# A fused attention and two-layer kernel: four output accumulators in step with the first product, transposes back on TensorE, batch 0 in quarters

## The chip, the cores and the metric

One core of a Trainium2 chip. The time is the device time of one execution in microseconds, as a median of several runs; beside it stands the span of a profiled execution, from the first to the last instruction.

## The reference, cut to what matters

```
B, H, S, Ns, D = 8, 8, 512, 32, 64          # x: B,H,S,D   state: B,H,Ns,D
scores  = x @ state^T / sqrt(D);  a  = softmax(scores)    # over the 32 states
xread   = a @ state
scores2 = state @ x^T / sqrt(D);  a2 = softmax(scores2)   # over the 512 rows
sread   = a2 @ x
rows    = concat(xread, sread) per batch -> (B*(S+Ns), H*D) = (4352, 512)
h = rows @ w_in                              # 512 -> 2048
g = 0.5*h*(1+erf(h/sqrt(2)))                 # exact gelu
out = g @ w_out                              # 2048 -> 512, float32
```

Inputs are float32, the kernel computes in bf16 with float32 accumulation. The kernel takes the softmax without subtracting the maximum.

## The kernel before, in words

Each batch has 512 x rows and 32 state rows. For the x rows the kernel never forms `xread`. It multiplies the state of a batch with `w_in` once (P, 256 x 2048, `pmat`, in four column blocks `f` of 512) and uses h = A P, where A is the softmax of the scores of all heads (512 x 256). `mm1(b, m)` makes 128 of the 2048 columns of h for all 512 rows (two matmuls of 512 columns) and ScalarE takes the gelu into `g`. The second product is cut into units of four matmuls: for one group j of 128 output rows and one quarter q of the 2048, so 16 units (`mm2`) a batch; after the quarter q = 3 DVE copies the bank out (`evac`) and SP stores 256 KB.

Attention of a batch: `rearr` puts x into `x4` (two heads side by side), x^T is made (`xT`), `scores` multiplies it with the block-diagonal state `sbd`, ScalarE takes exp into `e`, `norm` on DVE divides by the sum over states into `a`, and A^T (`AT`) is made. x^T and A^T come from TensorE transposes with a DVE copy (`xtr`, `atr`) for batches 0 and 1 and from transposing DMAs on SP (`xtr_dma`, `atr_dma`) for batches 2 to 7. `sread` multiplies e with x and with a column of ones, 64 matmuls of a 32x64 or 32x1 result; DVE divides; `srt` transposes the result into `XSR`. When all batches are through, `mm1_sr` and `mm2_sr` take the 256 state rows of all batches through the two products.

The order is written by hand. Batch 0 runs its attention in two halves with `keep_warm` matmuls in its gaps. Then a loop runs over 8 batches of 16 steps; step s runs what `extra` or `steady` list for it (the attention of the next batch and its P, two blocks at a time), then `mm1(b, s)`, then one `mm2` unit, 16 steps behind (`lag = 16`). So no unit runs during batch 0, and only two output banks are open at a time, one group j after another. The last eight units come after the state rows.

PSUM has eight banks. Pool `ps_f` has six of them, for everything but the output; `ps_o` has two, for the output and the warming matmuls. Each engine runs its own instructions in the order of the program. Weights, state and x of batches 1 to 7 come through POOL's software descriptors with a cast to bf16; x of batch 0 comes as float32 over SP and ACT in four pieces. Tiles `xb` have three buffers, so x of batch b + 3 is asked for when batch b has been rearranged.

Of the kernel before, what the change touches and what calls it, by code (L numbers as in the profile page):

```python
# [17 lines left out]
def kernel(  # L18
# [25 lines left out]
    ps_f = ctx.enter_context(tc.tile_pool(name="ps_f", bufs=6, space=bass.MemoryType.PSUM))  # L44
    ps_o = ctx.enter_context(tc.tile_pool(name="ps_o", bufs=2, space=bass.MemoryType.PSUM))
# [7 lines left out]
    ident = persist.tile([128, 128], BF16, name="ident")  # L53
    sbd = persist.tile([128, B, HC, 2 * NS], BF16, name="sbd")
# [4 lines left out]
    x0f = persist.tile([128, 2, HC, SJ * D], FP32, name="x0f")  # L59
    warm = persist.tile([128, 512], BF16, name="warm")  # L60
    ones = persist.tile([128, 1], BF16, name="ones")
    x4s = [persist.tile([128, SJ, HC, 128], BF16, name=f"x4_{i}") for i in range(2)]
# [5 lines left out]
    for c in range(HC):  # L68
        eng = nc.sync if c % 2 == 0 else nc.scalar
        eng.dma_start(out=x0f[:, :, c, :], in_=x0_rows[:, :, c, :])  # L70

    make_identity(nc, ident)
    nc.vector.memset(warm, 0.0)  # L73
    nc.gpsimd.memset(sbd, 0.0)
    nc.gpsimd.memset(ones, 1.0)
# [22 lines left out]
    load_w_in(0)  # L98
    load_w_in(1)
# [5 lines left out]
    load_w_in(2)  # L105
    load_w_in(3)
    load_w_out(0)
    load_w_out(1)
    load_x(2)
    load_w_out(2)  # L110
    load_w_out(3)
# [3 lines left out]
    def keep_warm(n):  # L115
        ps = ps_o.tile([128, 512], FP32, name="warm_ps", tag="op")
        for _ in range(n):
            nc.tensor.matmul(ps, lhsT=warm[:, 0:128], rhs=warm, start=True, stop=True)  # L118

# [25 lines left out]
    def begin(b):  # L145
        A = Att()
        atts[b] = A
        A.x4 = x4s[b % 2]
        A.xT = att.tile([128, SJ, HC, 128], BF16, name="xT", tag="xT")
        A.e = att.tile([128, SJ * 2, HC * NS], BF16, name="e", tag="e")  # L150
        A.a = att.tile([128, SJ * 2, HC * NS], BF16, name="a", tag="a")

    def rearr(b):
        A = atts[b]
        eng = nc.vector if b < 3 else nc.gpsimd
        for t in range(2):
            eng.tensor_copy(  # L157
                out=A.x4[:, :, :, 64 * t:64 + 64 * t].rearrange("p j c d -> p c j d"),
                in_=xbs[b][:, 4 * t:4 * t + 4, :].rearrange("p c (j d) -> p c j d", d=D),
            )  # L160

    def rearr0(c):
        A = atts[0]
        nc.vector.tensor_copy(
            out=A.x4[:, :, c, :].rearrange("p j (t d) -> p t j d", t=2),
            in_=x0f[:, :, c, :].rearrange("p t (j d) -> p t j d", d=D),
        )

    def xtr0(c):
        A = atts[0]  # L170
        ps = ps_f.tile([128, SJ, 128], BF16, name="xT_ps", tag="f")
        for j in range(SJ):
            nc.tensor.transpose(ps[:, j, :], A.x4[:, j, c, :], ident)
        nc.scalar.copy(out=A.xT[:, :, c, :], in_=ps)

    def xtr(b, half):
        A = atts[b]
        ps = ps_f.tile([128, 2, SJ, 128], BF16, name="xT_ps", tag="f")
        for ci in range(2):
            for j in range(SJ):  # L180
                nc.tensor.transpose(ps[:, ci, j, :], A.x4[:, j, 2 * half + ci, :], ident)
        nc.vector.tensor_copy(out=A.xT[:, :, 2 * half:2 * half + 2, :].rearrange("p j c n -> p c j n"), in_=ps)

    def score_mms(b, c):
        A = atts[b]
        if c % 2 == 0:
            A.pt = ps_f.tile([128, SJ, 2, 2, NS], FP32, name="pt", tag="f")
        for j in range(SJ):
            nc.tensor.matmul(  # L189
                A.pt[:, j, :, c % 2, :],  # L190
                lhsT=A.xT[:, j, c, :],
                rhs=sbd[:, b, c, :],
                start=True,
                stop=True,
            )

    def expo(b, half):
        A = atts[b]
        nc.scalar.activation(  # L199
            out=A.e[:, :, 64 * half:64 * half + 64],  # L200
            in_=A.pt.rearrange("p j t c n -> p (j t) (c n)"),
# [3 lines left out]

    def xtr_dma(b):
        A = atts[b]
        nc.sync.dma_start_transpose(
            out=A.xT.rearrange("p j c n -> p (j c) n"), in_=A.x4.rearrange("p j c n -> p (j c n)")
        )  # L210

    def scores(b, half):
        score_mms(b, 2 * half)
        score_mms(b, 2 * half + 1)
        expo(b, half)
# [17 lines left out]
    def atr(b):  # L233
        A = atts[b]
        A.AT = att.tile([128, SJ, 2, 128], BF16, name="AT", tag="AT")
        if b == 0:
            for t in range(2):
# [3 lines left out]
                o, i = A.AT[:, :, t, :], ps  # L241
# [9 lines left out]
        nc.vector.tensor_copy(out=A.AT.rearrange("p j t n -> p t j n"), in_=ps)  # L251

    def atr_dma(b):
        A = atts[b]
        A.AT = att.tile([128, SJ, 2, 128], BF16, name="AT", tag="AT")
        nc.sync.dma_start_transpose(
            out=A.AT.rearrange("p j t n -> p (j t) n"), in_=A.a
        )


    def sread(b):
        A = atts[b]
        sr = ps_f.tile([128, 130], FP32, name="sr", tag="f")
        for o, n in ((0, D), (128, 1)):
            for t in range(2):
                for j in range(SJ):
                    for c in range(HC):
                        q = slice(32 * c, 32 * c + 32)
                        nc.tensor.matmul(  # L269
                            sr[q, o + n * t:o + n * t + n],  # L270
                            lhsT=A.e[:, 2 * j + t, q],
                            rhs=A.x4[:, j, c, 64 * t:64 * t + 64] if n == D else ones,
                            start=(j == 0),
                            stop=(j == SJ - 1),
                        )
        A.srm = att.tile([128, 2, D], BF16, name="srm", tag="srm")
        inv = att.tile([128, 2], FP32, name="inv", tag="inv")
        nc.vector.reciprocal(out=inv, in_=sr[:, 128:130])
        nc.vector.tensor_tensor(
            out=A.srm,  # L280
            in0=sr[:, 0:128].rearrange("q (t d) -> q t d", t=2),
            in1=inv[:, :].to_broadcast((128, 2, D)),
            op=ALU.mult,
        )

    def srt(b):
        A = atts[b]
        ps = ps_f.tile([128, HC, NS], BF16, name="srT", tag="f")
        nc.tensor.transpose(
            ps.rearrange("p c n -> p (c n)"), A.srm.rearrange("q t d -> q (t d)"), ident  # L290
        )
# [4 lines left out]
    def pmat(b, fs, act=()):  # L296
        if b not in Ps:
            Ps[b] = att.tile([128, 2, d_ff], BF16, name="P", tag="P")
        pss = []
        for f in fs:  # L300
            ps = [ps_f.tile([128, 512], FP32, name="p_ps", tag="f") for t in range(2)]
            for c in range(HC):
                for t in range(2):
                    nc.tensor.matmul(  # L304
                        ps[t][32 * c:32 * c + 32, :],
                        lhsT=sbd[64 * t:64 * t + 64, b, c, 32 * t:32 * t + 32],
                        rhs=w_in_bf[64 * t:64 * t + 64, c, f * 512:(f + 1) * 512],
                        start=True,
                        stop=True,
                    )  # L310
            pss.append(ps)
        for f, ps in zip(fs, pss):
            for t in range(2):
                dst = Ps[b][:, t, f * 512:(f + 1) * 512]
                if (f, t) in act:
                    nc.scalar.copy(out=dst, in_=ps[t])  # L316
                else:
                    nc.vector.tensor_copy(out=dst, in_=ps[t])  # L318
# [4 lines left out]
    def mm1(b, m):  # L323
# [3 lines left out]
        for t in range(2):  # L327
# [3 lines left out]
                rhs=atts[b].AT[:, :, t, :],  # L331
# [20 lines left out]
    def mm2(u):  # L352
        b, r = u // 16, u % 16
        if b == 0:
            j, q = 2 * (r // 8) + r % 2, (r % 8) // 2
        else:
            j, q = r // 4, r % 4
        if q == 0:
            ops[j % 2] = ps_o.tile([128, d_model], FP32, name="op", tag="op")
        ps = ops[j % 2]  # L360
# [8 lines left out]
        if q == 3:  # L369
            rows = out[b * SB:b * SB + S, :].rearrange("(p j) n -> j p n", j=SJ)[j]  # L370
            evac(ps, [(rows, slice(0, 128))], last=(u == 16 * B - 1))
# [13 lines left out]
    def mm2_sr(s):  # L385
        ps = ps_o.tile([128, d_model], FP32, name="ops", tag="op")
# [18 lines left out]
    for c in range(HC):  # L405
        rearr0(c)
    xtr0(0)
    xtr0(1)
    score_mms(0, 0)
    xtr0(2)  # L410
    score_mms(0, 1)
    expo(0, 0)
    xtr0(3)
    score_mms(0, 2)
    keep_warm(2)
    score_mms(0, 3)
    expo(0, 1)
    norm(0, 0)
    norm(0, 1)
    keep_warm(6)  # L420
    pmat(0, (0,), act=((0, 0), (0, 1)))
    keep_warm(4)
    atr(0)
    keep_warm(2)

    extra = {
        0: {
            1: [lambda: pmat(0, (1,))],
            3: [lambda: state_prep(1, B)],
            5: [lambda: begin(1), lambda: rearr(1), lambda: xtr(1, 0)],  # L430
            6: [lambda: xtr(1, 1), lambda: scores(1, 0), lambda: scores(1, 1)],
            7: [lambda: pmat(0, (2,))],
            8: [lambda: norm(1, 0), lambda: norm(1, 1)],
            10: [lambda: pmat(0, (3,))],
            12: [lambda: pmat(1, (0,))],
            13: [lambda: atr(1)],
            14: [lambda: pmat(1, (1,))],
        },
        1: {
            1: [lambda: sread(0), lambda: pmat(1, (2,))],  # L440
            2: [lambda: srt(0)],
# [87 lines left out]
```

## Time and profile before

| | |
|---|---|
| median of 3 runs | 237.99 us (236.87 to 240.91) |
| profiled execution | 236.87 us |
| its span | 234.7 us |
| granted clock | 0.999 |
| first `mm1` starts | 14.59 us |
| first `mm2` unit starts | 31.45 us |
| last output copy starts | 230.70 us |

The page gives the busy time of each engine, the chain of work that ended last, the costliest groups of instructions, and the DMA issues. PE is TensorE's matmuls, PEld its weight loads, DVE VectorE, ACT ScalarE, POOL GpSimd, SP the queue of the sync engine. In a group, `out<-in` names the tiles; the number after `|` is busy time and mean of one; the last column is idle time ahead of it and what ended it. Three groups to know:

```profile
L335 ACT ACTIVATE g<-hp 128x512 bf16<-128x512 f32 x128 | 74.5, 602 | 61.9 <-PE hp L328 61.7
L318 DVE CAST P<-p_ps 128x512 bf16<-128x512 f32 x38 | 24.3, 684 | 11.1 <-PE p_ps L304 11.1
L376 PE MATMUL hps<-XSR,w_in_bf 128*128 128x256 bf16 x64 | 8.5, 273 | 0.0
```

The mean of a matmul is its length from first column to result; matmuls overlap, so what it costs in a dense row is the distance between starts.

### The profile page before, as it was taken

To read this page: it belongs to the slowest core of one execution; us is meant where nothing else is said; L and a number is where in the kernel's file an instruction comes from. 1 tells how busy PE (TensorE), PEld (TensorE's weight loads), DVE (VectorE), ACT (ScalarE), POOL (GpSimd) and SP (SyncE) were. 2 spreads that over 40 slices of the span, in tenths; PEclk is the share of its full clock that TensorE was granted. 3 is DMA by queue.
4 is the path that set the end of the run, shared out by engine and by line. 5 is a ranking of instruction groups with operands and counts; after the bars stand their busy time and mean duration, and the time that the engine had idled before them with its cause. 6 is when DMAs were issued, how large, how long until landed. Compare 5 with 4: busy or idle time off the path is not lost.

```text
span 234.7 us, 4315 instructions
## 1 busy us (share of the span) xinstructions
PE 217.1 (92%) x1844; PEld 100.7 (43%) x1844; DVE 85.3 (36%) x162; ACT 124.7 (53%) x208; POOL 28.1 (12%) x38
## 2 busy tenths in 40 slices
PE   5996799889979999999799999999999999999993
PEld 1543244434334444444344444444444444567441
DVE  2655974274135413631181317231623111111120
ACT  2577754485467446744494549454955454426000
POOL 8745001304000400030002000000000000000000
PEclk9999999999999999999999999999999999999999
DMA  7999999972923294252804061316131111211122
GB/s 205 149 178 206 202 205 185 126 161 26 226 76 86 56 165 98 62 75 53 128 0 106 31 143 38 89 47 134 46 92 45 47 45 55 80 46 47 27 65 87
DMA packets 38707, 23.12 MB, mean 98 GB/s; under 512 B 21920, under 2 KB 34464, under 8 KB 38688
## 3 DMA queue, kind: packets, MB, share of 16 engines
q0 software_dynamic: 13376, 8.09, 25.3%
q1 hardware_dynamic: 24352, 14.03, 24.8%
q10 hardware_dynamic: 960, 0.72, 1.0%
q8 instruction: 14, 0.23, 0.4%
q14 instruction: 5, 0.04, 0.1%
HBM read 17.30 MB, written 8.91 MB: 112 GB/s over the span
## 4 chain that ended last, share of the span: by engine, by line
PE 68%; DMA 18%; DVE 5%; ACT 3%; POOL 3%; issue 1%; SPq 1%; POOLq 0%; ACTq 0%
PE op L362 37%; PE hp L328 18%; DMA xT<-x 13%; DMA xb<-in_x_dram 5%; PE hps L376 3%; PE ops L388 3%; PE p_ps L304 3%; PE sr L269 2%; PE pt L189 2%; ACT g L335 2%; DVE osb L348 1%; POOL w_in_bf L79 1%; DVE P L318 1%; DVE a L226 1%; DVE cs L223 1%
## 5 line engine op out<-in xcount | busy, mean ns | idle before, releaser
L362 PE MATMUL op<-w_out_bf,g 128*128 128x512 bf16 x512 | 130.2, 379 | 0.0
L335 ACT ACTIVATE g<-hp 128x512 bf16<-128x512 f32 x128 | 74.5, 602 | 61.9 <-PE hp L328 61.7
L328 PE MATMUL hp<-AT,P 128*128 128x512 bf16 x256 | 75.9, 380 | 2.9 <-DVE P L318 1.5
L362 PEld LDWEIGHTS <-g 128*128 128x128 bf16 x512 | 50.1, 98 | 58.7
L348 DVE COPY osb<-op 128x512 f32<-128x512 f32 x31 | 21.4, 690 | 88.8 <-PE op L362 88.8
L328 PEld LDWEIGHTS <-P 128*128 128x128 bf16 x256 | 22.5, 98 | 30.2 <-issue 6.6
L318 DVE CAST P<-p_ps 128x512 bf16<-128x512 f32 x38 | 24.3, 684 | 11.1 <-PE p_ps L304 11.1
L157 POOL COPY x<-xb 128x1024 bf16<-128x1024 bf16 x10 | 10.1, 1044 | 93.3 <-PE sr L269 76.9
L316 ACT CAST P<-p_ps 128x512 bf16<-128x512 f32 x26 | 14.1, 601 | 6.1 <-PE p_ps L304 6.1
L223 DVE TENSOR_REDUCE cs<-e 128x16 f32<-128x512 bf16 x16 | 10.9, 682 | 17.2 <-ACT e L199 17.2
L199 ACT ACT_TABLE_LOAD x7 | 9.0, 1283 | 9.7 <-PE pt L189 9.7
L189 PE MATMUL pt<-sbd,xT 128*128 128x64 bf16 x128 | 6.3, 200 | 6.2 <-DMA xT<-x 5.4
L304 PE MATMUL p_ps<-w_in_bf,sbd 64*32 64x512 bf16 x256 | 11.9, 384 | 0.1
L226 DVE TENSOR_TENSOR a<-e,ics 128x512 bf16<-128x512 bf16 x16 | 11.1, 692 | 0.6
L383 ACT ACTIVATE g_sr<-hps 128x256 bf16<-128x256 f32 x16 | 6.1, 384 | 8.4 <-PE hps L376 8.0
L335 ACT ACT_TABLE_LOAD x8 | 10.3, 1283 | 0.1
L189 PEld LDWEIGHTS <-xT 128*128 128x128 bf16 x128 | 4.9, 102 | 10.5 <-DMA xT<-x 8.4
L199 ACT ACTIVATE e<-pt 128x512 bf16<-128x512 f32 x16 | 8.8, 595 | 0.7 <-PE pt L189 0.6
L118 PE MATMUL warm_ps<-warm 128*128 128x512 bf16 x20 | 7.9, 542 | 1.2 <-DVE warm L73 1.2
L376 PE MATMUL hps<-XSR,w_in_bf 128*128 128x256 bf16 x64 | 8.5, 273 | 0.0
L345 ACT COPY osb<-op 128x256 f32<-128x256 f32 x1 | 0.4, 372 | 13.9 <-DVE osb L343 13.9
L376 PEld LDWEIGHTS <-w_in_bf 128*128 128x128 bf16 x64 | 6.3, 98 | 2.7
(48 smaller groups left out, 81.8 us busy)
## 6 DMA issues: line engine op xcount, KB each, us to landing
out_dram<-osb SPq DMA_DIRECT2D x31, 256.0 KB, 2.3
xb<-in_x_dram POOLq DMA_DIRECT2D x7, 512.0 KB, 11.6
w_in_bf<-in_moe_w_in_dram POOLq DMA_DIRECT2D x8, 256.0 KB, 10.1
w_out_bf<-in_moe_w_out_dram POOLq DMA_DIRECT2D x4, 512.0 KB, 14.9
x0f<-in_x_dram SPq DMA_DIRECT2D x2, 256.0 KB, 3.4
x0f<-in_x_dram ACTq DMA_DIRECT2D x2, 256.0 KB, 4.3
out_dram<-osb SPq DMA_DIRECT2D x8, 64.0 KB, 1.7
st_bf<-in_state_dram POOLq DMA_DIRECT2D x1, 224.0 KB, 10.2
```

Of the source, the lines that this page charges most:

```text
L189: nc.tensor.matmul(A.pt[:, j, :, c % 2, :], lhsT=A.xT[:, j, c, :], rhs=sbd[:, b, c, :], start=True, stop=True,)
L199: nc.scalar.activation(out=A.e[:, :, 64 * half:64 * half + 64], in_=A.pt.rearrange("p j t c n -> p (j t) (c n)"), func=AF.Exp, scale=scale,)
L223: nc.vector.reduce_sum(out=cs, in_=e4, axis=AX.X)
L226: nc.vector.tensor_tensor(out=A.a[:, :, hs].rearrange("p g (c n) -> p g c n", n=NS), in0=e4, in1=ics[:, :, :].to_broadcast((128, G, 2, NS) ...
L304: nc.tensor.matmul(ps[t][32 * c:32 * c + 32, :], lhsT=sbd[64 * t:64 * t + 64, b, c, 32 * t:32 * t + 32], rhs=w_in_bf[64 * t:64 * t + 64, c ...
L316: nc.scalar.copy(out=dst, in_=ps[t])
L318: nc.vector.tensor_copy(out=dst, in_=ps[t])
L328: nc.tensor.matmul(hp, lhsT=Ps[b][:, t, m * 128:(m + 1) * 128], rhs=atts[b].AT[:, :, t, :], start=(t == 0), stop=(t == 1),)
L335: nc.scalar.activation(out=gs[b][:, m, :], in_=hp, func=AF.Gelu)
L348: nc.vector.tensor_copy(out=osb, in_=ps)
L362: nc.tensor.matmul(ps, lhsT=gs[b][:, m, j * 128:(j + 1) * 128], rhs=w_out_bf[:, m, :], start=(m == 0), stop=(m == MC - 1),)
L376: nc.tensor.matmul(hp, lhsT=w_in_bf[:, c, m * 128:(m + 1) * 128], rhs=XSR[:, c, :], start=(c == 0), stop=(c == HC - 1),)
```

## The change

- PSUM: four banks in each pool. The four groups j of a batch have an output bank each; units run by quarter (q, then j), so that a unit needs only the gelus of its quarter. `lag` is 5 instead of 16. `mm2_sr` takes its bank from `ps_f`.
- Batch 0 is written out as a list with units between the `mm1`s; `w_out` chunks are loaded alternately with `w_in` blocks.
- Batch 0's attention goes by pairs of heads (`scores0`, `norm0`), half of its x comes over POOL with a cast (`x0b`), and a small gelu (`gate`) stands after the last exp.
- `xtr` and `atr` on TensorE for all batches; the transposing DMAs are gone. `xT` and `AT` change their layout to fit.
- `sread` is 4 matmuls of 260 columns for each half t, with a column of ones inside `x4` (now 132 wide) and all heads against all heads; DVE divides and masks with `hmask`. `srt` gathers with four matmuls against `istack`.
- `pmat` does one block at a time, with one or both of its casts on ScalarE where `act` says so. Blocks 1 to 3 of batch b are made in batch b's own steps 1, 5 and 9.
- The state rows' first product is interleaved with batch 7.

```diff
-    ps_f = ctx.enter_context(tc.tile_pool(name="ps_f", bufs=6, space=bass.MemoryType.PSUM))
-    ps_o = ctx.enter_context(tc.tile_pool(name="ps_o", bufs=2, space=bass.MemoryType.PSUM))
+    ps_f = ctx.enter_context(tc.tile_pool(name="ps_f", bufs=4, space=PSUM))
+    ps_o = ctx.enter_context(tc.tile_pool(name="ps_o", bufs=4, space=PSUM))
...
-    for c in range(HC):
-        eng = nc.sync if c % 2 == 0 else nc.scalar
-        eng.dma_start(out=x0f[:, :, c, :], in_=x0_rows[:, :, c, :])
+    for c in range(2):
+        nc.sync.dma_start(out=x0f[:, :, c, :], in_=x0_rows[:, :, c, :])
+    nc.vector.memset(warm, 0.0)
+    for c in range(2):
+        nc.gpsimd.dma_start(out=x0b[:, :, c, :], in_=x0_rows[:, :, 2 + c, :])
...
-    nc.gpsimd.memset(sbd, 0.0)
+    nc.vector.memset(sbd, 0.0)
...
-    load_w_in(0)
-    load_w_in(1)
+    for f in range(2):
+        load_w_in(f)
+        load_w_out(f)
...
-    load_w_in(2)
-    load_w_in(3)
-    load_w_out(0)
-    load_w_out(1)
+    for f in range(2, FC):
+        load_w_in(f)
+        load_w_out(f)
     load_x(2)
-    load_w_out(2)
-    load_w_out(3)
     load_x(3)
...
+    nc.vector.reduce_sum(
+        out=hmask, in_=ident.rearrange("p (c n) -> p c n", n=NS), axis=AX.X
+    )
...
+    def scores0(c):
+        A = atts[0]
+        A.pc = ps_o.tile([128, SJ, 2, NS], FP32, name="pc", tag="op")
+        for j in range(SJ):
+            nc.tensor.matmul(
+                A.pc[:, j, :, :], lhsT=A.xT[:, c, j, :], rhs=sbd[:, 0, c, :], start=True, stop=True
+            )
+        nc.scalar.activation(
+            out=A.e[:, :, NS * c:NS * c + NS],
...
-    def xtr_dma(b):
-        A = atts[b]
-        nc.sync.dma_start_transpose(
-            out=A.xT.rearrange("p j c n -> p (j c) n"), in_=A.x4.rearrange("p j c n -> p (j c n)")
-        )
...
+    def sread(b, t):
...
+        sr = ps_f.tile([128, HC, 65], FP32, name="sr", tag="f")
+        for j in range(SJ):
+            nc.tensor.matmul(
+                sr,
+                lhsT=A.e[:, 2 * j + t, :],
+                rhs=A.x4[:, j, :, 1 + 65 * t:66 + 65 * t],
+                start=(j == 0),
+                stop=(j == SJ - 1),
+            )
+        d0, one = (1, 0) if t == 0 else (0, 64)
+        inv = att.tile([128, 1], FP32, name="inv", tag="inv")
+        nc.vector.reciprocal(out=inv, in_=sr[:, 0, one:one + 1])
+        nc.vector.scalar_tensor_tensor(
+            out=A.srm[:, :, t, :],
+            in0=sr[:, :, d0:d0 + 64],
+            scalar=inv,
+            in1=hmask[:, :].to_broadcast((128, HC, D)),
+            op0=ALU.mult,
+            op1=ALU.mult,
         )
...
-        nc.tensor.transpose(
-            ps.rearrange("p c n -> p (c n)"), A.srm.rearrange("q t d -> q (t d)"), ident
-        )
+        for c in range(HC):
+            nc.tensor.matmul(
+                ps[:, c, :],
+                lhsT=A.srm[:, c, :, :].rearrange("q t d -> q (t d)"),
+                rhs=istack,
+                start=True,
+                stop=True,
+            )
...
+    def mm2(b, q, j):
         if q == 0:
-            ops[j % 2] = ps_o.tile([128, d_model], FP32, name="op", tag="op")
-        ps = ops[j % 2]
+            ops[b, j] = ps_o.tile([128, d_model], FP32, name="op", tag="op")
+        ps = ops[b, j]
...
+    scores0(3)
+    nc.scalar.activation(out=gate, in_=hmask, func=AF.Gelu)
+    norm0(2)
+    norm0(3)
     keep_warm(2)
-    score_mms(0, 3)
...
+    pmat(0, 0, act=(1,))
+    keep_warm(3)
     atr(0)
...
+    M(0, 1, 2, 3)
+    U((0, 0), (0, 1))
+    pmat(0, 1)
+    U((0, 2))
+    M(4)
+    U((0, 3))
+    M(5)
+    sread(0, 0)
+    M(6)
+    sread(0, 1)
+    M(7)
+    srt(0)
+    U((1, 0))
+    state_prep(1, B)
+    begin(1)
+    rearr(1)
+    U((1, 1))
+    xtr(1, 0)
+    xtr(1, 1)
+    U((1, 2))
+    scores(1, 0)
+    scores(1, 1)
+    U((1, 3))
+    pmat(0, 2, act=(1,))
+    norm(1, 0)
+    norm(1, 1)
+    sread(1, 0)
+    M(8)
+    sread(1, 1)
+    M(9, 10)
+    srt(1)
+    M(11)
+    U((2, 0))
+    atr(1)
...
+    pmat(1, 1)
+    M(14, 15)
+    for j in range(SJ):
+        U((3, j))
+        M(16 + j)
+    begin(2)
+    rearr(2)
+    load_x(4)
+
+    lag = 5
+
+    def plan(b):
+        nb = b + 1
+        d = {}
+        if b > 1:
+            d[1] = [lambda: pmat(b, 1, act=(0, 1))]
+            if nb < B:
+                d[0] = [lambda: begin(nb), lambda: rearr(nb)]
+                if b + 3 < B:
+                    d[0].append(lambda: load_x(b + 3))
+        d[5] = [lambda: pmat(b, 2)]
+        d[9] = [lambda: pmat(b, 3)]
+        if nb < B:
+            d[4] = [lambda: xtr(nb, 0)]
+            d[5].append(lambda: xtr(nb, 1))
+            d[8] = [
+                lambda: scores(nb, 0),
+                lambda: scores(nb, 1),
+                lambda: norm(nb, 0),
+                lambda: norm(nb, 1),
+            ]
+            d[10] = [lambda: sread(nb, 0)]
+            d[11] = [lambda: sread(nb, 1)]
+            d[12] = [lambda: srt(nb)]
+            d[13] = [lambda: pmat(nb, 0)]
+            d[14] = [lambda: atr(nb)]
+        else:
+            for k in range(MC):
+                d.setdefault(k, []).append(lambda k=k: mm1_sr(k))
         return d
...
+    for b in range(1, B):
+        d = plan(b)
+        for k in range(4 if b == 1 else 0, MC):
+            for f in d.get(k, ()):
+                f()
+            mm1(b, k)
+            if 16 * b + k - lag >= 16:
+                Us(16 * b + k - lag)
+    Us(16 * B - 5)
     mm2_sr(0)
     mm2_sr(1)
-    while u < 16 * B:
-        mm2(u)
-        u += 1
+    for j in range(SJ):
+        Us(16 * B - 4 + j)
```

## The prediction

> **What bounds the kernel now.** I read the front page first, then the chain of work that ended last, then the waits, then the instructions in order of time in one steady batch.
>
> ```profile
> span 234.7 us, 4315 instructions
> PE 217.1 (92%) x1844; PEld 100.7 (43%) x1844; DVE 85.3 (36%) x162; ACT 124.7 (53%) x208; POOL 28.1 (12%) x38
> PEclk9999999999999999999999999999999999999999
> PE 68%; DMA 18%; DVE 5%; ACT 3%; POOL 3%; issue 1%; SPq 1%; POOLq 0%; ACTq 0%
> ```
>
> TensorE is busy for 92% of the span at a full granted clock, and it leads the chain. An added TensorE instruction therefore costs its own time unless it falls into one of the gaps. The gaps sum to 17.6 us (234.7 - 217.1).
>
> The prices are starts of successive pieces of the chain of waits (start, duration, what), taken over 18 to 60 us:
>
> ```profile
> 20.37 0.46 PE xT_ps L181 x8
> 29.00 0.45 PE aT_ps L250 x8
> 29.87 0.34 PE p_ps L304 x8
> 37.90 0.63 PE sr L269 x61
> 44.76 0.64 PE pt L189 x16
> 45.40 0.43 PE hp L328 x2
> 45.83 0.86 PE op L362 x4
> ```
>
> So eight 128-column transposes hold TensorE for 0.46 us, one column block of P 0.34, a batch's state read 0.63, its scores 0.64, one `mm1` 0.432 and one `mm2` unit 0.864.
>
> ```profile
> 115.33 0.64 PE L189 MATMUL pt<-sbd,xT 128*128 128x64 bf16 x16 [1.44 <-DMA xT<-x]
> 115.81 1.28 ACT L199 ACT_TABLE_LOAD   x1 [2.15 <-PE pt L189]
> 117.10 1.09 ACT L199 ACTIVATE e<-pt 128x512 bf16<-128x512 f32 x2
> 118.21 1.28 ACT L335 ACT_TABLE_LOAD   x1
> 119.50 1.57 ACT L335 ACTIVATE g<-hp 128x512 bf16<-128x512 f32 x3
> ```
>
> Here TensorE stands 1.44 us for the transposing DMA, and ScalarE then gives no gelu from 115.81 to 120.10: load, two exps, load, first gelu. Six PSUM buffers let TensorE run on meanwhile.
>
> ```profile
> PE pt L189 <- DMA xT<-x: 5.4, 6, 1.8
> PE hp L328 <- DVE P L318: 1.5, 4, 0.8
> PE hp L328 <- ACT g L335: 1.0, 1, 1.0
> ```
>
> The waits (total, times, longest) say what the removed DMAs are worth on TensorE: 5.4 us.
>
> **TensorE's own work, before.** 128 units x 0.864 = 110.6; 128 `mm1` x 0.432 = 55.3; the state rows' products 7.0 + 6.9; scores 8 x 0.64 = 5.1; P: 8 single blocks x 0.34 and 12 pairs x 0.56 = 9.4; state reads 8 x 0.63 = 5.0; transposes and the rest 3.7. Sum 203.0. The span adds 12.1 us of the head (the first `mm1` is at 14.59, 2.5 of this work lies before it), 4.0 from the last matmul (230.66) to the end, and so 15.6 of waits after 14.59.
>
> **What the change adds to it.** Batches 2 to 7 transpose x (16) and A (8) on TensorE: 6 x 24 x 0.0575 = 8.3. P goes one block at a time: 12 x (0.68 - 0.56) = 1.4. The state read becomes 8 matmuls of 260 columns a batch. No such shape is in the trace: 128 columns take 0.0575, 512 take 0.216, and the nearest, 256 columns (L376, 0.44 for 4), 0.11. I take 0.11, so 0.88 against 0.63: +2.0 in all (ends -1.4 and +8.8). `srt` becomes four 32-column matmuls instead of one transpose; by the 64-column scores (0.04 each) and the transposes (0.0575) it is 0.16 to 0.23 for 0.06, +1.2. In all +12.9, TensorE's work is 216. The selectors `hmask` and `istack`, two small DVE reductions before any x has landed, are hidden by the wait for state (DVE idle until 4.05); without that cover they cost some 0.5 us.
>
> *A page beside the row.* The Trainium skill, "TensorE: Matmul & The Clock Gate", section "Back-to-back issue gap", puts a stream of weight load and matmul pairs at N=128 at about 81 ns each; the trace has 57.5. By the page the 144 transposes would be 11.7 us instead of 8.3. Against that, "VectorE: DVE Perf Modes", section "The three transpose paths", gives 390 ns for a 128x128 on TensorE and 1309 ns by DMA and prefers TensorE, which counts latency; in this trace the DMA's time is spent off the busiest engine and only 5.4 us of it is waited for.
>
> **Steady batch, after.** Work: 16 x 1.296 = 20.7, scores 0.64, state read 0.88, P 4 x 0.34 = 1.36, transposes 1.38, `srt` 0.2: 25.2 us, where the cycle before is 24.2 with its waits (scores at 115.33 and 139.54). The fewer banks decide what is waited for. I followed the releaser of each of the 32 banks that a batch takes from `ps_f`. From the start of the scores, TensorE has `pt` twice 0.64, `mm1` 0.43, a unit 0.86, P 0.34, `mm1` 0.43, a unit 0.86: 3.56 us. Then the state read needs the bank whose gelu is the first after the exps. That gelu ends 0.48 + 1.28 + 1.09 + 1.28 + 0.6 = 4.75 after the start, by the rows above, and 0.06 passes until TensorE moves: a wait of 1.26 us (part of it already at P and the `mm1` after it, whose banks the exps release). Next in line are two P casts on DVE behind both `norm`s (3.3 us from the first exp, 117.73 to 121.04, then 0.68): the first ends at 6.3, the bank is wanted at 6.6, covered by 0.3 us. The four output banks are free in time, their copies (0.69 each) come one per 1.3 us and the next batch wants the first bank over 5 us after its copy could start. Queued behind the waiting state read are only TensorE's own instructions. SP loses its 12 transposing DMAs (2 to 4 us of issue each) and holds stores alone; POOL's rearrangement waits for the state read of two batches earlier, as now.
>
> So a steady batch is 25.2 + 1.3 = 26.5 us, six times (batches 1 to 6): 7.6 of waits. Batch 7 interleaves the state rows' first product; ScalarE needs 0.5 + 0.38 of every 1.73, no wait.
>
> **Head.** Loads: SWDGE lands 256 KB each 1.4 us, 512 KB each 2.55 (9.05 for the first `w_in` piece, 26.1 and 28.6 for two `w_out` chunks), a stream that stays full until 40. Ahead of it now go two small pieces of x; POOL gives up the 1.8 us memset. The two pieces land at 5 to 6 by that rate, against 5.5 for their ACT-queue predecessors; if software descriptors take as long as the first weight piece (6.0 from issue), 7 to 8. New order by the stream: `w_in`0 8.8, `w_out`0 11.3, `w_in`1 14.1, `w_out`1 16.7, state 18.5, x1 21.1, then two blocks of weights by 32: none is wanted earlier. Quarters: the last exp ends near 9.9, four `norm0` on DVE (about 0.85 each) end at 12.4, where the halves ended at 12.56; then A^T 0.5, its copies 0.5, first `mm1` at 13.7 (14.59 before), and the gelu table load is behind it thanks to `gate`.
>
> From 13.7 on I walk the written list: work to the end of `M(19)` is 20 `mm1` 8.6, 16 units 13.8, five P blocks 1.7, state reads and `srt` 2.2, transposes, scores, state preparation 2.4: 28.8. Waits: the second P block's cast before `M(4)` 0.5; `srt` 0.3; unit (1,0) on the last of four gelus 0.6; `xtr(1,0)` on DVE (two state copies 1.26, two rearrangements 0.84) 1.5; `sread(1,0)` on the exps 1.0; gelu table load before `M(10)` and the unit after it 1.0; P casts before `M(15)` 0.6: 5.5. End at 48.0. Then `xtr(2,0)` waits for the last output copy and `rearr(2)` on DVE: 1.2.
>
> **Sum.** 48.0 + 1.2 + remaining work (108 `mm1` 46.7, 112 units 96.8, state rows 13.9, six attentions 18.6, 26 P blocks 8.8: 184.8) + 7.6 = 241.6. The end has four stores within 3 us instead of two, but the last half copies hang on the last matmul as now: 4.0 (to 5). Span 245.6; the profiled execution took 236.87, 2.2 above its span, so 247.8; the median of the runs is 1.1 above that execution: 249.
>
> **Rivals.**
> 1. *Banks and DVE, worse.* If the 0.3 us of cover behind the `norm`s is gone (a DVE step some tenths longer), `mm1` and the second state read wait for P casts too: up to 1.1 a batch more, 256. For: DVE is the queue with most steps there; against: each price is a row.
> 2. *Late head.* x by software descriptors lands at 8 and moves everything by 2 to 3 us: 252.
> 3. *The waits go, not slower.* Early units fill the head's gaps, the fixed order fits, and the bank wait is hidden: with all 14.3 us of waits gone, 216 + 11.3 + 4.0 = 231.3 of span, 235 as a median. It decides when the waits fall below about 8 (2% above 237.99 is 242.7). For: 15.6 us of waits exist to be taken; against: the length of ScalarE's exp stretch is made of rows, and six banks become four.
> 4. *Does not do what it says*: if the second product started no earlier, the head's waits would be 2 us more; inside the range.
>
> **Numbers.** Forecast 0.62, rivals 0.16, 0.1, 0.1, 0.02. Low end 243: half of the new waits; high end 256: rival 1. A measurement of this kernel tells about 2% from no change: slower 0.86, within 0.12, faster 0.02, since even without any wait the time is 235.
>
> **What would show it.** The profile after should have fewer matmuls (the small state reads go: some 1556 for 1844) yet more work: scores 26 to 27 us apart, waits of the state read or of P on ScalarE's gelu and exp near 1.3 us a batch, no wait on a DMA for x^T, first `mm1` near 13.7. The forecast is wrong if scores come under 25 us apart, if 260-column matmuls are far from 0.11, or if the first unit waits for `w_out`.

## The result and the profile after

| kernel | median of 4 runs, us | lowest to highest | profiled execution | its span |
|---|---|---|---|---|
| before | 238.86 | 236.87 to 240.91 | 236.87 | 234.7 |
| changed | 251.66 | 250.95 to 253.06 | 251.88 | 249.7 |

The changed kernel takes 1.0572 times as long, interval 1.0474 to 1.0671: slower. The forecast was 249.0 (243 to 256).

The front page of the changed kernel: span, busy time by engine, the granted TensorE clock in forty slices, the shares of the chain that ended last, and two of its costliest groups.

```profile
span 249.7 us, 3755 instructions
PE 230.6 (92%) x1555; PEld 109.7 (44%) x1555; DVE 112.7 (45%) x222; ACT 120.7 (48%) x198; POOL 28.0 (11%) x38
PEclk9679999999999999999999999999999999999997
PE 75%; ACT 12%; DVE 5%; DMA 4%; issue 1%; POOL 1%; SPq 0%; ACTq 0%; DVEq 0%; POOLq 0%
L293 PE MATMUL sr<-x,e 128*128 128x260 bf16 x64 | 10.0, 277 | 2.7 <-ACT g L363 2.7
L228 PE MATMUL xT_ps<-ident,x 128*128 128x128 bf16 x112 | 8.5, 220 | 2.3 <-DVE x L170 2.3
```

TensorE has 289 matmuls fewer and is still busy for 13.5 us more (230.6 against 217.1), nearly all of the 15.0 us that the span grew. In the chain, DMA falls from 18% to 4% and ScalarE rises from 3% to 12%: the wait for a transfer is gone, and a wait for an activation has come. The clock line has two digits below 9 near the start, which the page of before has not.

The waits of TensorE in the changed kernel (total, times, longest):

```profile
PE sr L293 <- ACT g L363: 2.7, 6, 0.5
...
PE srT L316 <- DVE srm L303: 2.3, 2, 2.0
PE xT_ps L228 <- DVE x L170: 2.3, 2, 1.3
...
PE p_ps L334 <- ACT e L244: 0.9, 5, 0.2
...
PE p_ps L334 <- DMA w_in_bf<-in_moe_w_in_dram: 0.8, 2, 0.7
```

No line names the transfer of x^T. The first comes once in each steady batch, the fourth in five of the six. The instructions of one such batch in order of time (start, duration, and in brackets the idle time before):

```profile
136.32 0.63 PE L237 MATMUL pt<-sbd,xT 128*128 128x64 bf16 x16
136.79 0.60 PE L356 MATMUL hp<-AT,P 128*128 128x512 bf16 x2
137.22 1.03 PE L386 MATMUL op<-w_out_bf,g 128*128 128x512 bf16 x4
138.18 0.39 PE L334 MATMUL p_ps<-w_in_bf,sbd 64*32 64x512 bf16 x1
138.74 0.41 PE L334 MATMUL p_ps<-w_in_bf,sbd 64*32 64x512 bf16 x7 [0.18 <-ACT e L244]
139.23 0.59 PE L356 MATMUL hp<-AT,P 128*128 128x512 bf16 x2
139.66 1.02 PE L386 MATMUL op<-w_out_bf,g 128*128 128x512 bf16 x4
141.14 0.62 PE L293 MATMUL sr<-x,e 128*128 128x260 bf16 x4 [0.45 <-ACT g L363]
```

From the start of the scores to the state read are 4.82 us. Read by starts, the work between them is 3.4: scores 0.47, `mm1` 0.43, unit 0.86, P 0.34, `mm1` 0.43, unit 0.86. So TensorE stands for 1.4 us: the P block holds it for 1.05 (138.18 to 139.23) instead of 0.34, the unit ahead of the state read for 1.48 (139.66 to 141.14) instead of 0.86, and the P block starts 0.1 late. The forecast had 3.56 of work and 1.26 of wait, because it took the scores at 0.64, their time to the last result; the next `mm1` starts 0.47 after them, here and in the kernel before. The brackets show only half of the wait, since a listed duration runs on beside the next instruction; starts are the safer reading. The same stretch in the chain of waits is the forecast's own list, table load, two exps, table load, first gelu:

```profile
136.80 1.28 ACT L244
138.09 1.09 ACT e L244 x2
139.20 1.28 ACT L363
140.49 0.61 ACT g L363
141.14 0.62 PE sr L293 x4
```

The kernel before has a small wait of the same kind in each batch, which the forecast passed over: with six banks its first pair of P blocks and the `mm1` behind it wait for the first two gelus after the exps, and the pair holds TensorE for 0.85 us by starts, against 0.56 for the other pair.

```profile
119.86 0.24 PE p_ps L304
120.10 0.50 ACT g L335
120.59 0.04 issue
120.64 0.59 PE hp L328 x2
```

### The profile page after: what moved, and what is told of

It reads as the page before. It is cut to its first block, busy times and chain, and to the rows that moved or that the text cites. A ratio compares the mean times of both kernels' runs of the same rounds, so it can differ in the third digit from the quotient of the medians.

```text
span 249.7 us, 3755 instructions
## 1 busy us (share of the span) xinstructions
PE 230.6 (92%) x1555; PEld 109.7 (44%) x1555; DVE 112.7 (45%) x222; ACT 120.7 (48%) x198; POOL 28.0 (11%) x38
## 3 DMA queue, kind: packets, MB, share of 16 engines
q0 software_dynamic: 13920, 8.36, 24.2%
## 4 chain that ended last, share of the span: by engine, by line
PE 75%; ACT 12%; DVE 5%; DMA 4%; issue 1%; POOL 1%; SPq 0%; ACTq 0%; DVEq 0%; POOLq 0%
PE op L386 37%; PE hp L356 19%; PE p_ps L334 4%; ACT L363 3%; ACT L244 3%; PE sr L293 3%; ACT g L363 3%; PE hps L400 3%; PE xT_ps L228 3%; DMA w_in_bf<-in_moe_w_in_dram 3%; PE ops L412 3%; ACT e L244 3%; PE aT_ps L284 1%; DVE P L346 1%; DMA out_dram<-osb 1%
## 5 line engine op out<-in xcount | busy, mean ns | idle before, releaser
L346 DVE CAST P<-p_ps 128x512 bf16<-128x512 f32 x49 | 31.6, 684 | 22.9 <-PE p_ps L334 22.8
L257 DVE TENSOR_REDUCE cs<-e 128x16 f32<-128x512 bf16 x14 | 9.5, 681 | 26.7 <-ACT e L244 26.7
L334 PE MATMUL p_ps<-w_in_bf,sbd 64*32 64x512 bf16 x256 | 15.9, 393 | 1.7 <-ACT e L244 0.9
L293 PE MATMUL sr<-x,e 128*128 128x260 bf16 x64 | 10.0, 277 | 2.7 <-ACT g L363 2.7
L334 PEld LDWEIGHTS <-sbd 64*32 64x32 bf16 x256 | 4.1, 89 | 17.8 <-issue 15.5
L344 ACT CAST P<-p_ps 128x512 bf16<-128x512 f32 x15 | 8.2, 588 | 7.4 <-PE p_ps L334 7.4
L228 PE MATMUL xT_ps<-ident,x 128*128 128x128 bf16 x112 | 8.5, 220 | 2.3 <-DVE x L170 2.3
L229 DVE COPY xT<-xT_ps 128x1024 bf16<-128x1024 bf16 x14 | 9.5, 682 | 1.4 <-PE xT_ps L228 1.4
L260 DVE TENSOR_TENSOR a<-e,ics 128x512 bf16<-128x512 bf16 x14 | 9.7, 692 | 0.5
L293 PEld LDWEIGHTS <-e 128*128 128x128 bf16 x64 | 6.1, 96 | 8.1 <-issue 4.4
```

Of the source, the lines that this page charges most:

```text
L260: nc.vector.tensor_tensor(out=A.a[:, :, hs].rearrange("p g (c n) -> p g c n", n=NS), in0=e4, in1=ics[:, :, :].to_broadcast((128, G, 2, NS) ...
L293: nc.tensor.matmul(sr, lhsT=A.e[:, 2 * j + t, :], rhs=A.x4[:, j, :, 1 + 65 * t:66 + 65 * t], start=(j == 0), stop=(j == SJ - 1),)
L334: nc.tensor.matmul(ps[t][32 * c:32 * c + 32, :], lhsT=sbd[64 * t:64 * t + 64, b, c, 32 * t:32 * t + 32], rhs=w_in_bf[64 * t:64 * t + 64, c ...
```

## The experiments

The common yardstick is the time from one batch's scores to the next batch's, batches 3 to 7, read from the starts of the `pt` matmuls. It leaves the head and the tail out.

| kernel | cycles, us | span of the profiled execution |
|---|---|---|
| before | 24.22, 25.19, 24.21, 24.16 | 234.7 |
| changed | 26.14, 26.67, 26.67, 26.67 | 249.7 |
| before, transposes on TensorE | 24.93, 24.93, 24.92, 24.88 | 235.8 |
| before, x^T asked for earlier | 23.60, 23.58, 23.58, 23.54 | 232.8 |
| changed, P block ahead of the scores | 25.35, 25.72, 25.72, 25.73 | 246.5 |
| changed, state reads of before | 25.80, 26.32, 26.32, 26.28 | 247.6 |
| changed, state reads a step later | 26.11, 26.63, 26.64, 26.63 | 250.9 |
| changed, two parts undone | 24.46, 24.99, 24.99, 24.95 | 236.2 |
| changed, three parts undone | 23.76, 24.38, 24.36, 23.73 | 232.0 |

(One cycle in some rows is about half a microsecond shorter than its neighbours; the others are compared.)

**1. The kernel before with TensorE's transposes.** The six batches whose x^T and A^T came by DMA use the kernel's own `xtr` and `atr` instead.

```diff
...
-        d[0].append(lambda: xtr_dma(nb))
+        d[3] = [lambda: xtr(nb, 0), lambda: xtr(nb, 1)]
...
-        d[8] = [lambda: atr_dma(nb)]
+        d[8] = [lambda: atr(nb)]
```

> The kernel before, with x^T and A^T of batches 2 to 7 made on TensorE (x^T in step 3, in batch 1 in step 7; A^T in step 8) and all else as it was. Theory (priced work): 144 transposes x 0.0575 = 8.3 us more on TensorE, less the 5.4 us it stood for the DMA and about 1 us of smaller waits: +2 to +3 us, a span near 237. Rival (the transposes are most of the whole difference of 13 us): +8 us or more, a span of 243 or above. Rival (the DMA waits were worth more than the transposes): faster than before.

238.61 us against 236.01, ratio 1.0116 (1.0051 to 1.018). No wait on a transfer is left, and the cycle is 24.9. Its chain of waits now holds the sixteen transposes of x, and no transfer ahead of the scores:

```profile
112.71 0.89 PE xT_ps L181 x16
...
114.90 0.47 PE pt L189 x16
```

The exchange costs work in every batch and saves a wait that was long in three of the six (0.9 to 1.8 us by the brackets, 0.45 in the others).

**2. The kernel before with x^T asked for earlier.** Rearrangement, load and DMA move from step 0 of a batch to step 15 of the one before it, for batches 3 to 7.

```diff
-        d[0] = [lambda: begin(nb), lambda: rearr(nb)]
...
-        d[0].append(lambda: xtr_dma(nb))
+        if nb + 1 < B:
+            d[15] = [lambda: begin(nb + 1), lambda: rearr(nb + 1)]
...
+            d[15].append(lambda: xtr_dma(nb + 1))
```

> The kernel before, with rearrangement, load and the transposing DMA of x^T put one step earlier, ahead of the store that stands in front of it on SP (step 15 of the batch before instead of step 0). Theory: the 5.4 us that TensorE stood for x^T go, because the DMA starts some 5 us sooner: 4 to 6 us faster than before, a span of 229 to 231. Rival (another wait stands behind it, such as the gelu after the exps): less than 2 us.

233.12 us against 236.01, ratio 0.9829 (0.9748 to 0.991): the only version here whose interval lies below the kernel before. It gains 2.9 us where the theory had 4 to 6: the waits on x^T fall from 5.4 to 2.4. The cycle of 23.58 (experiment 3 has the same) has no wait on x^T, so it is a clean base: 24 transposes a batch on TensorE cost 24.92 - 23.58 = 1.34 us, and the waits that they replace were worth 24.2 - 23.58 = 0.6 in three of the four cycles listed and 1.6 in the fourth. Batch 2, whose request was not moved, still waits:

```profile
PE pt L189 <- DMA xT<-x: 2.4, 2, 2.2
```

**3. The same, and batch 2's request two steps earlier.**

```diff
-            3: [lambda: pmat(1, (3,)), lambda: begin(2), lambda: rearr(2), lambda: xtr_dma(2)],
+            1: [..., lambda: begin(2), lambda: rearr(2), lambda: xtr_dma(2)],
+            3: [lambda: pmat(1, (3,))],
```

> The kernel before, with x^T of batches 3 to 7 asked for one step earlier as in the run above, and x^T of batch 2 two steps earlier (step 1 of batch 1, right behind the state read that frees its buffer). Theory: the 2 us that TensorE still stood for x^T of batch 2 go too, a span of 229 to 231. Rival (x of batch 2 has not landed, DVE then stands in front of P's casts): no gain over the run above.

232.33 us (231.63 to 234.08); the kernel before took 234.04 to 240.52 in the same session, too scattered for a ratio. The wait did not go (3.0 us in all, longest 2.7), so the theory missed and asking earlier is not what batch 2 lacks. Asked for at 35.98 us, the transfer landed 10.9 us later; asked for at 39.67 in experiment 2, 7.6 later. The loads were still running, two of x until 40.0 and 44.1. Whether they hold the transfer was not tried.

**4. The changed kernel, fourth P block ahead of the scores.**

```diff
-        d[9] = [lambda: pmat(b, 3)]
+        d[7] = [lambda: pmat(b, 3)]
```

> The changed kernel, with the fourth column block of P made in step 7 instead of step 9, so that no P block takes banks between the scores and the state read. Theory (the new wait is the four banks during ScalarE's load, exps, load): from the scores to the state read TensorE then has more work than banks to wait for, about 1.1 us a batch goes, six times: 6 to 7 us less, a span near 243, and the state read no longer waits for a gelu. Rival (the next wait is DVE's, the P casts and norms): less than 2 us gained, with waits on DVE in place of those on ScalarE.

248.72 us against 236.01, ratio 1.0524 (1.0472 to 1.0576). The cycle loses 0.95 us and the state read waits for nothing:

```profile
136.38 0.63 PE L237 MATMUL pt<-sbd,xT 128*128 128x64 bf16 x16
136.85 0.60 PE L356 MATMUL hp<-AT,P 128*128 128x512 bf16 x2
137.28 1.03 PE L386 MATMUL op<-w_out_bf,g 128*128 128x512 bf16 x4
138.14 0.59 PE L356 MATMUL hp<-AT,P 128*128 128x512 bf16 x2
138.57 1.03 PE L386 MATMUL op<-w_out_bf,g 128*128 128x512 bf16 x4
139.44 0.62 PE L293 MATMUL sr<-x,e 128*128 128x260 bf16 x4
...
143.33 0.27 PE L316 MATMUL srT<-istack,srm 128*128 128x32 bf16 x4 [0.20 <-DVE srm L303]
```

From the scores to the state read are now 3.06 us, the 3.4 of above less the P block's 0.34. With the P block's two banks out of the stretch, four banks last until the gelus resume. Part of the gain is given to the next wait in line, `srT` behind DVE's normalising: the unit ahead of it holds TensorE for 1.23 instead of 0.86, so 1.33 of waiting go and 0.37 come. The span fell by 3.2 us, not by the 5.7 of six cycles: in this execution the second batch's transposes began at 53.40 instead of 51.11, of which 1.1 had come by the scores of batch 1 (30.74 for 29.68) and the rest behind a stretch of half clock (last section).

**5. The changed kernel, both state reads one step later.** The sum alone doesn't say whether the wait belongs to the state read or to the banks.

```diff
-            d[10] = [lambda: sread(nb, 0)]
-            d[11] = [lambda: sread(nb, 1)]
-            d[12] = [lambda: srt(nb)]
-            d[13] = [lambda: pmat(nb, 0)]
+            d[11] = [lambda: sread(nb, 0)]
+            d[12] = [lambda: sread(nb, 1)]
+            d[13] = [lambda: srt(nb)]
+            d[13].append(lambda: pmat(nb, 0))
```

> The changed kernel with both state reads and the state row's transposing products one step later, behind one more mm1. Theory (four ps_f banks and ScalarE's load, exp, load stretch): whichever tile comes fourth after mm1 number 8 has to wait for that bank's gelu, and this is now mm1 number 10 in place of the state read; the wait of about 1.1 us a batch changes its name to one of hp on ACT g, scores stay 26.5 to 26.9 us apart, span 249 to 251. Rival (the wait belongs to the state read, which is asked for too early): it goes away, scores about 25.6 apart, span about 243.

One run, 253.12 us (before: 239.63), span 250.9. The cycle stays at 26.63. The same idle time, to the hundredth, stands ahead of the `mm1` that now comes fourth:

```profile
140.55 0.59 PE L356 MATMUL hp<-AT,P 128*128 128x512 bf16 x2
140.98 1.02 PE L386 MATMUL op<-w_out_bf,g 128*128 128x512 bf16 x4
142.46 0.59 PE L356 MATMUL hp<-AT,P 128*128 128x512 bf16 x2 [0.45 <-ACT g L363]
```

So the wait is that of the bank, whoever asks for it.

**6. The changed kernel with the state reads of before.** The small matmuls return, and the ones columns leave x's rows.

```diff
-        sr = ps_f.tile([128, HC, 65], FP32, name="sr", tag="f")
-        for j in range(SJ):
...
+        sr = ps_f.tile([128, 130], FP32, name="sr", tag="f")
+        for o, n in ((0, D), (128, 1)):
+            for t in range(2):
+                for j in range(SJ):
...
```

> The changed kernel, with the state read and its transpose as before (64 small matmuls into one bank, one transpose, x4 without its columns of ones). Theory: 8 x (0.92 - 0.63) + 8 x 0.03 = 2.6 us less on TensorE, and one bank fewer taken a batch: 2 to 4 us less, a span of 246 to 248. Rival (the new form pays by fewer instructions): no change or slower.

249.57 us against 236.01, ratio 1.0557 (1.0486 to 1.0629). The cycle loses 0.35 us. Fewer and wider matmuls were the slower form here: 64 instructions a batch took 0.63 to 0.70 us in one piece, the 8 that replace them 0.46 for each four, and `srt` went from 0.06 to about 0.09.

**7 and 8. Two and three parts undone together.** Both have the DMA transposes and the state reads of before in the changed kernel's order; the second has the P block ahead of the scores too.

```diff
+                d[0].append(lambda: xtr_dma(nb))
...
-            d[4] = [lambda: xtr(nb, 0)]
-            d[5].append(lambda: xtr(nb, 1))
...
-            d[14] = [lambda: atr(nb)]
+            d[10].append(lambda: atr_dma(nb))
```

> As the run with three things undone, but the fourth P block stays behind the scores as in the changed kernel. Theory: 26.67 - 1.35 - 0.35 = 25.0 us between scores, with the state read waiting for the first gelu after the exps; the wait belongs to the banks, not to the transposes. Rival (the wait came from DVE's copies of the transposes): 24.3 or less.

> The changed kernel's order, lag, four output banks and head, with three things undone in batches 2 to 7: x^T and A^T by the transposing DMA (x^T asked for at step 0, A^T at step 10), state reads as before (in all batches), and the fourth P block ahead of the scores. Theory (the terms add up): per batch 26.67 - 1.35 - 0.35 - 0.95 = 24.0 us between scores, no wait on the DMA, since eight steps lie between x^T's request and the scores; six batches 16 us less than the changed kernel, plus 0.6 for batches 0 and 1: a span of 232 to 235, level with the kernel before. Rival (the four banks or the lag of five cost by themselves): cycles of 25 us or more, a span above 238.

Two undone: one run, 238.3 us, cycle 24.99 for the theory's 25.0. TensorE's waits still hold 2.7 us over six times of the state read behind ScalarE's gelu, the sum of the changed kernel: the transposes have no part in it. Three undone: 234.82 us (233.86 to 235.67) in the session where before took 234.04 to 240.52; not told apart from before. Its cycle is 23.73 to 23.76 in two batches and 24.4 in two (24.0 in the theory), and the longer ones have a new wait, here in order of time on TensorE and then on DVE:

```profile
109.68 0.23 PE L329 MATMUL srT<-ident,srm 128*128 128x128 bf16 x1 [0.43 <-DVE srm L319]
```

```profile
107.71 1.51 DVE L259 TENSOR_TENSOR a<-e,ics 128x512 bf16<-128x512 bf16 x1
109.14 0.16 DVE L318 RECIPROCAL inv<-sr 128x2 f32<-128x2 f32 x1
```

The normalising product takes 1.51 us here and 0.69 everywhere in the changed kernel (the last section comes back to it).

**9. The changed kernel, TensorE kept busy until the first weights land, and six output tiles.**

```diff
-    keep_warm(2)
+    keep_warm(10)
     pmat(0, 0, act=(1,))
...
-    opool = ctx.enter_context(tc.tile_pool(name="opool", bufs=4))
+    opool = ctx.enter_context(tc.tile_pool(name="opool", bufs=6))
```

> The changed kernel, with ten warming matmuls instead of two ahead of the first P block and six output tiles instead of four. Theory (head and tail terms): TensorE was left idle for the first w_in block and its granted clock then stood at half from about 8 to 15 us; kept busy, the clock holds and the first product of batch 0 starts 0.5 to 1 us sooner; at the end the last copy no longer waits 0.58 us for an output tile. In all 1 to 2 us less, a span near 248. Rival (the half clock covers only time in which DVE and the loads set the pace): the first product starts where it did, only the 0.6 us at the end go.

252.85 us (252.41 to 253.13), no gain; the theory missed. The granted clock of the head was 1.00, but so it was in experiments 4 to 6, which have the two warming matmuls of the changed kernel, so this run does not show that ten of them hold it. And they outlast the landing of the weights (9.90): the first P block starts behind them at 13.13, the first `mm1` at 15.03 instead of 14.23, and the second batch's transposes at 51.62 instead of 51.11. Whether fewer of them would gain was not tried. At the end, the last copy's wait for an output tile fell from 0.58 to 0.17:

```profile
245.17 0.43 DVE L371 COPY osb<-op 128x256 f32<-128x256 f32 x1 [0.17 <-DMA out_dram<-osb]
```

From the last matmul to the end it is still 5.3 us (5.1 in the changed kernel): the last store lands 3.5 us after the last matmul in both, so the stores set the end, not the tile.

## Why the prediction was right, point by point

**Steady batch: 26.5 forecast, 26.67 measured.** The mechanism is the one forecast: the state read stands for the bank whose gelu comes first after the exps, 4.82 us from the scores for 4.81. (The forecast's terms for that gelu add up to 4.73, not 4.75.) Experiments 4 and 5 show it: take two banks out of the stretch and the wait goes, exchange the tiles' order and it stays under another name. The transposes cost 1.34 a batch (forecast 1.38). The 260-column matmul took 0.115 for the estimated 0.11, near its neighbour of 256 columns; `srt` took 0.1 for 0.2. That the sum is right to 0.2 is in part luck, since terms with errors of opposite sign meet in it: the scores hold TensorE for 0.47 and not 0.64, so the work is smaller and the wait 1.4 and not 1.26. And the forecast left out that a P block behind a unit starts 0.1 late (0.96 after the unit's start for 0.86), four times a batch now; before, each of two pairs and the state read did so.

**Where 2.47 us a batch went** (26.67 - 24.2): transposes +1.34, transfers no longer waited for -0.6, state reads +0.35 (each shown by a run), and by the starts in the two profiles the wait for banks 1.33 now and 0.29 before, +1.04, P in single blocks +0.24 (1.36 for 1.12) and one late start more, +0.1. Moving the P block gains 0.95 of the wait, as experiment 4 shows. Over the five cycles from batch 2's scores to batch 7's this makes 13.9 of the 15.0 us by which the span grew. All that lies ahead of them and behind them, with the second product's early start, makes the other 1.1: batch 2's scores start 12.1 us later than before, and from batch 7's to the end it is 11.0 us less.

**The transfers.** The part of the change that removes the DMA transposes buys nothing. Experiment 1 prices it alone at +1.2% (0.5 to 1.8), and experiment 2 shows that the wait it removes could be had by asking earlier.

**Head: the forecast was 1.9 us short.** The step "`w_in`0 8.8" failed: the first P block waited for two pieces of these weights until 10.0 and 11.2, as the head in order of time shows.

```profile
10.01 0.60 PE L334 MATMUL p_ps<-w_in_bf,sbd 64*32 64x512 bf16 x1 [0.20 <-DMA w_in_bf<-in_moe_w_in_dram]
11.27 0.63 PE L334 MATMUL p_ps<-w_in_bf,sbd 64*32 64x512 bf16 x7 [0.65 <-DMA w_in_bf<-in_moe_w_in_dram]
11.82 1.46 PE L123 MATMUL warm_ps<-warm 128*128 128x512 bf16 x3
13.08 1.06 PE L274 MATMUL aT_ps<-ident,a 128*128 128x128 bf16 x8
14.23 2.34 PE L356 MATMUL hp<-AT,P 128*128 128x512 bf16 x8
```

The first `mm1` starts at 14.23 for 13.7. In experiments 4 and 5, whose head is the same program, other steps are late: the second piece landed at 10.1 and 10.8, but the last of the four `norm0` ended at 13.5 (forecast 12.4), and the first `mm1` came at 14.64 and 14.53. From the first `mm1` of the changed kernel to the end of `M(19)` 35.7 us passed for 34.3 forecast: 0.45 of it is the half clock (four `mm1` in 2.18 us instead of 1.73), and a wait of 2.0 that the walk did not have, `srT` of batch 1 behind two `norm`s and two `srm` on DVE, leaves the other 0.9 net of what others took less. The wait before the second batch's transposes was 1.2, as forecast.

**Tail: 5.1 us, forecast 4.0 "(to 5)".** Experiment 9 puts it down to the stores.

**Sum.** The span is 4.1 us over the forecast 245.6: head 1.9, the stretch from 51.1 to the last matmul 1.1 (193.5 for 192.4), tail 1.1. What lies around the span was 2.2, as taken. The forecast then added 1.1 for the median over the profiled execution, and the median came out 0.2 below it. So the number is off by 2.7 us where the span is off by 4.1: that part is luck.

**The rivals.** 1, P casts late behind the `norm`s: not in the changed kernel (no such wait in its steady batches), but their neighbour, `srT` behind `srm`, comes when the bank wait goes (experiment 4, and the longer cycles of 8). 2, x late by software descriptors: x landed 3.9 us after its issue, by 5.9; in this execution it was the weights that came late. 3, the waits go: those on transfers went, and the bank wait took their place. 4 does not hold: the first unit of the second product starts at 16.41, behind the fourth `mm1`.

## What to carry to other kernels

Where a transfer is waited for, first ask for it earlier; its work given to the engine that bounds the kernel is paid in every batch. PSUM banks are time: where an engine falls silent for a known stretch (here two table loads and two exps, 4.8 us), count the tiles that are asked for in it and the banks that come free in it. Seven tiles on four banks, of which the exps free two, made a wait of 1.3 us, whatever tile came last. To tell a wait of an instruction from a wait of its buffer, exchange two neighbours: if the wait stays in its place, it is the buffer's.

## What the runs showed of the hardware

**The granted clock halved for 3 to 7 us in some executions and not in others.** In the changed kernel it was 0.50 to 0.55 from 8 to 14 us. In experiment 5 it fell after the same wait for `srm` at 36.7 that passed without it in the changed kernel. Two stretches of that run (start:end, length, busy us of PE, PEld, DVE, ACT, POOL, then the granted clock, DMA share and GB/s), and then its chain of waits behind the pause:

```profile
34.00:38.00 4.00, 1.86 (x10) 0.70 (x10) 2.82 (x8) 1.50 (x4) 0.00 (x0) 0.89 1.46 197
38.00:42.00 4.00, 4.00 (x27) 1.86 (x26) 1.01 (x2) 0.56 (x2) 2.89 (x3) 0.69 0.65 90
```

```profile
36.73 0.27 PE srT L316 x4
36.99 0.66 PE hp L356 x2
37.65 1.71 PE op L386 x4
39.36 0.85 PE aT_ps L284 x8
```

A unit took 1.71 us instead of 0.86 and eight transposes 0.85 instead of 0.45; the next batch's scores start at 58.28 instead of 56.84, which covers the difference of the two spans (1.2). Such stretches lay at 37.5 to 41 us in experiment 4 and 36.5 to 40 in experiment 6, near 20 to 24 and 48 to 51 in experiment 2, at 7.5 to 11 in experiments 1 and 3 and 7.5 to 14 in the kernel with three parts undone, and nowhere in the profile of before until its last matmul was done. In the head such a stretch need not cost: the first `mm1` came at 14.23 with it in the changed kernel and at 14.53 without it in experiment 5. Nor does the clock line show all slow matmuls: in experiment 4, from 15.6 to 16.9 us, those of the head's `mm1` start 0.43 us apart instead of 0.22, without a wait, while it reads 1.00. What decides whether a pause brings a slow stretch was not found.

**GpSimd's copies beside VectorE.** In experiment 8 the rearranging copies on POOL fell on DVE's normalising products. In three of the four batches where they overlapped, one product took 1.51 us instead of 0.69, and those of these batches that lie in the cycles listed are the cycles of 24.4 (23.7 without). In each of the three the copy had started less than 0.1 us ahead of the product. In the fourth the product started first, by 0.03: it took 0.69, and the copy 1.57 instead of 1.04. In the changed kernel the copies overlap only the last 0.2 us of a product, and all of these take 0.69. The Trainium skill, "SBUF — State Buffer", section "SBUF: two separate sides", says that a VectorE operation with two inputs in SBUF and a GpSimd operation that reads SBUF share a pair of ports, and that the one that starts later is held for the whole of the other's instruction. The rows agree in order and in size: the later one is held, the product by 0.82, within one copy of 1.04, the copy by 0.53, within one product of 0.69. It was not tried by itself.
